# Attention and expert layer on one core: the attention's hand-planned order drawn up anew, with longer landing times of its DMA transpositions and loads

## The chip, the cores and the metric

The kernel runs on one core of a Trainium2 chip. The metric is the device time in microseconds of one execution, as the median of several runs; the kernel before takes 1341.63 us (three runs, 1341.21 to 1343.16). The engines of the core issue independently, each strictly in its own order, and wait for each other by semaphores: TensorE (PE in the profile, PEld for its weight loads), VectorE (DVE), ScalarE (ACT), GpSimd (POOL) and SyncE (SP), which here only issues DMAs.

## What is computed

An attention over 8 batches x 8 heads (576 positions of width 64) in which each query keeps its 32 largest scores, followed by a layer of eight experts, to which the 4608 tokens are assigned greedily by their gate's logits, with 576 tokens for each expert.

```python
def _attn_ref(q, k, v):                      # (8, 8, 576, 64) each
    scores = np.matmul(q, k.transpose(0, 1, 3, 2)) / np.sqrt(64)
    kth = np.partition(scores, -32, axis=-1)[..., -32:-31]
    scores = np.where(scores >= kth, scores, -1e9)
    attn = np.exp(scores - np.max(scores, axis=-1, keepdims=True))
    attn = attn / (np.sum(attn, axis=-1, keepdims=True) + 1e-09)
    return np.matmul(attn, v)

x = attention.transpose(0, 2, 1, 3).reshape(4608, 512)
# logits = x @ w_gate; pairs (token, expert) in falling order, 576 tokens an expert
out[token] = np.maximum(x[token] @ w1[e], 0) @ w2[e]
```

## The kernel before

The attention takes the heads in 32 pairs (`pairs`; index `n`), and a pair's queries in nine tiles of 128 rows: tiles 0 to 3 belong to the first head, 5 to 8 to the second, and tile 4 holds the 64 rows that are left of each. Values are split in a high and a low half of 16 bits, so that products of 16-bit numbers give the precision of 32 bits.

**Preparing a pair** (`prep`, lines 355 to 428, for pairs 1 to 31). SP loads keys and queries (`ldk`, `ldq`: lines 364 and 365, two DMAs each; `ldq` may not start ahead of `ldk`) and values (`ldv`, `ldw`: lines 368 and 370). ACT rounds the keys to 16 bits (`hk`, line 379) and the queries (`hq`, 378); POOL scales both (`gk`, `gq`, 383) and subtracts the rounded part, which gives the lower parts (`lk`, `lq`, 384). Then SP transposes the keys by DMA into `Kt` (`tk`, line 394, which needs `hk` and `lk`) and the queries into `Qt` (`tq`, line 394, which needs `hq` and `lq`). POOL copies a corner of `Kt` into `kz` (`kz`, line 396), and splits the values (`hv` 371, `gv` 374, `lv` 375). Both transpositions must have landed before the first scores of the pair.

**A tile** (`tile_ops`, line 429). PE computes the scores into PSUM (`s0`, `s1`, line 449); DVE takes the eight largest of each of six pieces (`c0` to `c5`, lines 453 and 454) and ranks the 48 candidates (`k0` to `k4`, lines 457 to 461); ACT marks by sign which scores exceed the 24th and counts them (`nt` 462, `sg` 466); DVE turns the count into a fill (`fl`, 476); PE takes the marked scores away (`o0`, `o1`, lines 471, 472 and 449, the latter with `kz`); DVE finds the next eight (`y8`, line 473) and ACT keeps what is left (`rl`, 479). After three tiles POOL copies their maxima into the query tile (`mo`, line 500) and SP transposes them (`q2`, line 501).

**The weights of a tile** (`soft`, line 503). PE adds up the transposed scores and masks (`ma`, `mb` 515; `ag0` to `ag3`, 520 and 521), ACT takes the exponential into a buffer `F` or `E` (`ex`, 525; `F` has four buffers in rotation), POOL splits it (`eh` 528, `el` 531; `el` frees the buffer). `tail` does the same for the last 64 keys (`tm` to `tc`, `te`, `th`, `tl`), `values` (line 597) multiplies with the values (`v0` to `v2`), `logits` computes the gate's logits for the pair.

**What sets the order.** Every operation is entered with a due time: the entry of the table `TAU` for its name and tile, plus `n` times `PER`. The last pair has entries of its own (with `_`). `Loom.run` (line 144) sorts each engine's operations by due time and lets the engine issue them in exactly that order; a due time is a place in the order, and delays nothing by itself. The planner keeps a clock of its own beside it, from the duration `d` and the landing time `late` (the time between the end of the issue and the use) of each operation. This clock decides the order in which the engines' instructions are written into the program and how many filling products PE gets in planned gaps (`stay`, line 346). The routing's first part is put behind the last pair (`pa`, `pb`). Then the expert layer follows with a planner of its own.

```python
        for op in sorted(self.ops, key=lambda o: o["t"])[::-1]:
            if op["e"]: lines[op["e"]].append(op)
```

Of the kernel before, what the change touches and what calls it, by code (L numbers as in the profile page):

```python
# [210 lines left out]
def attention(tc, q,k,v,w_gate,x_out,L,acc,cuts, pairs,ahead=()):  # L211
# [3 lines left out]
    with ExitStack() as ctx:  # L215
# [7 lines left out]
        V,G,A,T=nc.vector,nc.gpsimd,nc.scalar,nc.tensor  # L223
# [34 lines left out]
        def rims():  # L258
# [8 lines left out]
        PER=24.535894  # L267
        TAU=dict(ldk=[-36.532489], ldq=[-34.645812], hk=[0.490652], gk=[-24.714477], lk=[-5.646046], cq=[-5.038599], hq=[4.011956], gq=[-18.2134], lq=[-1.41611], tk=[-9.773551], 
            tq=[-4.444251], kz=[-1.095786], ldv=[-24.423458], ldw=[-15.183043], hv=[1.708939], gv=[1.465658], lv=[25.618464], 
            s0=[15.009426,17.614268,18.631424,22.361038,24.496034,25.814059,27.254638,33.349677,36.178074],   # L270
            s1=[16.343093,17.885021,20.327135,22.783661,26.664804,25.913004,28.409475,33.746851,36.209416], 
            c0=[15.654456,17.929975,19.415024,22.536798,25.246239,26.257597,28.63835,34.277851,36.041556], 
            c1=[17.465533,19.354973,19.526392,23.324677,26.510292,27.491491,30.464787,35.252934,36.134791], 
            c2=[16.14122,19.028081,20.113037,23.116345,26.52603,27.664486,31.6479,34.660167,36.642377], 
            c3=[17.439299,18.346588,19.614338,22.878597,26.109616,28.666317,30.753739,34.412699,36.484631], 
            c4=[17.433128,19.11846,19.726728,23.098966,25.671467,26.710686,30.311069,34.875005,36.785795], 
            c5=[17.596633,18.81432,20.666021,23.663524,27.350852,28.872828,29.897138,34.293634,36.846704], 
            k0=[17.656568,19.718444,21.338341,23.830734,27.576103,30.498137,31.893452,35.844752,37.524856], 
            k1=[17.901067,19.816894,21.373417,24.48664,28.321978,31.388234,31.971058,36.583722,38.053143], 
            k2=[18.064263,20.452465,21.832022,24.637402,28.778187,31.776554,32.244806,37.313756,38.482906],   # L280
            k3=[18.993761,21.078023,21.844845,25.194363,28.998044,31.961926,32.319626,38.002729,40.436698], 
            k4=[19.074582,21.339742,22.085206,25.227026,29.974125,32.191951,32.957171,38.220581,41.56231], 
            nt=[19.923862,21.07989,21.635673,25.254182,28.591256,32.027101,35.264635,38.85557,41.390678], 
            sg=[20.428927,21.387458,23.353451,27.967037,31.229058,33.065454,36.668009,40.650797,41.58337], 
            fl=[21.577768,23.681133,25.061496,28.688352,31.777369,33.560239,37.442546,41.651365,42.368937], 
            o0=[22.255713,23.476629,23.782874,29.486798,31.978369,34.185679,39.17079,40.855488,42.489752], 
            o1=[22.580295,23.758687,24.695984,29.602817,32.243463,35.167978,39.421143,40.990239,42.794684], 
            y8=[23.918204,24.466854,25.583237,31.427866,32.292299,35.365448,39.778219,42.173235,43.421626], 
            rl=[24.524765,24.674952,25.985548,31.889713,33.167469,37.480824,40.938297,43.094705,44.212375], mo=[17.22803,22.609648,32.244558], q2=[11.61061,18.819227,22.679302], 
            ma=[28.187642,28.949286,34.490254,37.224887,36.588764,41.036568,47.11078,43.383667,46.883924],   # L290
            mb=[28.23947,29.200388,34.68484,38.173395,37.181707,41.348337,47.186607,43.395459,47.135361], 
            ag0=[28.394948,29.705353,35.236427,38.677025,37.486884,41.916796,47.782677,43.90671,47.273045], 
            ag1=[28.459302,30.02036,35.766277,38.717047,37.66623,42.06767,48.090036,43.991452,47.55756], 
            ag2=[28.761553,30.046327,35.893568,38.829728,37.866094,42.091054,48.175398,44.686062,47.642137], 
            ag3=[28.897045,30.35191,35.899376,39.091561,38.127979,42.704103,48.27918,45.03561,47.820927], 
            ex=[30.703735,31.866723,36.101128,38.52712,38.229268,43.764389,48.909161,45.107316,48.482621], 
            eh=[30.707012,25.992076,30.410065,32.650788,0,35.796509,42.676563,41.704942,42.62945], 
            el=[33.507947,35.037032,32.484109,35.292126,0,36.976438,45.999822,46.502435,46.867538], cu=[43.086149], tm=[45.201666], tn=[45.828976], ta=[46.475366], tb=[46.487846], 
            te=[45.579953], th=[37.430026], tl=[41.594999], tc=[48.93781], tr=[49.863139], v0=[48.332202,48.464061,48.800604,49.234735,49.265037,49.318516,49.731533,50.138756], 
            n0=[50.382659], i0=[50.679088], x0=[50.554385,51.338797,51.396623,52.155786], v1=[50.538791,50.772288,51.395036,51.76531,51.787905], n1=[52.080784], i1=[52.839633],   # L300
            x1=[52.866022], v2=[55.191767,55.935243,56.126953,56.189534,57.051874,57.720408,57.831705,57.842499], n2=[57.42161], i2=[58.184646], 
            x2=[58.08899,58.376986,58.610975,60.544343], lt0=[64.108659], lt1=[64.320988], lt2=[64.321728], lt3=[65.107349], lc=[66.399674], ld0=[67.432455], ld1=[67.437679], 
            ld2=[67.516612], ld3=[67.572664], lp=[68.382371], rt0=[63.984394], rc=[63.180125], rd0=[64.630251], rd1=[65.022487], rp=[66.272452], st=[73.135698], ldk_=[-35.889897], 
            ldq_=[-35.188398], hk_=[0.616827], gk_=[-24.933336], lk_=[-5.038599], cq_=[-2.708316], hq_=[3.883817], gq_=[-20.049088], lq_=[0.195792], tk_=[-9.504837], tq_=[-4.870748], 
            kz_=[8.382132], ldv_=[-15.700575], ldw_=[-12.925284], hv_=[1.695369], gv_=[11.624079], lv_=[41.595099], 
            s0_=[14.912706,17.433233,18.631324,20.492929,24.453667,25.169692,26.759069,32.243563,35.872581], 
            s1_=[15.007788,17.854586,19.373458,21.992311,25.725414,26.77937,28.395048,34.185579,36.064346], 
            c0_=[15.536163,17.833143,19.614438,21.338441,24.723626,25.671567,26.799064,32.717003,35.943152], 
            c1_=[15.943341,19.702662,19.748862,23.522126,25.570329,25.678257,29.603343,32.771706,37.189612], 
            c2_=[16.351868,19.714023,20.612321,22.341619,24.926231,25.769041,28.558249,32.776643,36.041656],   # L310
            c3_=[17.439199,18.520609,20.318569,23.023736,25.194363,26.143094,27.405455,34.195478,37.584804], 
            c4_=[15.843145,19.604253,19.960156,23.738631,25.227026,25.852663,31.296853,32.8259,38.666525], 
            c5_=[15.715676,19.746815,20.561277,23.584636,25.922609,27.350852,30.641257,34.449493,37.7529], 
            k0_=[17.533337,20.305911,21.471646,24.034479,26.591582,27.638632,33.08639,35.365448,39.723553], 
            k1_=[17.656568,20.452465,21.577868,24.123414,26.916815,30.182078,33.972607,36.785795,40.096054], 
            k2_=[18.064163,20.610546,21.890349,24.43491,27.267468,30.99811,34.365495,38.053143,40.397585], 
            k3_=[18.648077,20.943324,22.268027,24.637402,27.491591,31.970958,35.156304,39.458481,41.787164], 
            k4_=[19.614338,21.373417,22.792541,25.42924,27.664486,32.243382,35.844652,39.778219,41.857785], 
            nt_=[19.923862,20.954933,23.353451,25.362363,28.111171,31.3086,35.264635,40.289699,41.800716], 
            sg_=[20.234342,22.563689,23.830252,25.725512,30.106172,33.065454,37.551336,40.654704,42.614537],   # L320
            fl_=[21.832022,23.081535,23.955728,27.266875,30.540837,35.252834,41.302682,42.882482,42.882582], 
            o0_=[22.083337,23.307503,23.743286,28.180748,32.214938,35.994341,39.561765,42.194735,42.684328], 
            o1_=[22.509549,23.601583,23.862297,28.720863,32.243463,36.058538,40.2929,42.539638,42.789509], 
# [16 lines left out]
            pb_=[0,0,0,0,0,0,0,0,96.391443,0,0,121.358085,0,0,0,0,0,121.468485])  # L340
# [14 lines left out]
        def prep(n):  # L355
# [61 lines left out]
            def go(name,*a,**kw): return at((n,name,0),*a,**kw)  # L417
# [11 lines left out]
        def tile_ops(P,i):  # L429

            n=P["n"]
            def go(name,*a,i=i,**kw): return at((n,name,i),*a,**kw)
# [987 lines left out]
```

## Time and profile before

| what | value |
|---|---|
| median of three runs | 1341.63 us |
| the profiled execution, its own time | 1338.39 us |
| its span, first to last instruction | 1336.6 us |
| PE busy | 1242.4 us (93%) |
| DVE busy | 1096.9 us (82%) |
| ACT busy | 929.5 us (70%) |
| POOL busy | 818.5 us (61%) |
| mean granted clock of TensorE | 0.968 of full speed |

The attention takes the span to about 885 us; the expert layer follows. All times are in us from the span's start unless marked. A row of the timeline is one instruction, or several alike in a row (x2 and so on): its start, its duration, engine, line, operation, output<-input, shape, and in brackets how long the engine stood idle before it and whose work ended that. For SP the duration is that of issuing; the data lands later, which is seen at the instruction whose wait "DMA Kt<-nk" or "DMA Qt<-nq" ends. A row by stretches gives the length of the stretch, the busy time (and count) of each engine in it, the granted TensorE clock, the busy share of the DMA engines, and GB/s.

### The profile page before, as it was taken

Reading aid. Unit: us, or ns where it says so; the run is one execution under the profiler, and the core shown is the slowest. Engines: PE = TensorE matmul, PEld = TensorE weight load, DVE = VectorE, ACT = ScalarE, POOL = GpSimd, SP = SyncE. Lnnn points to the kernel's source line nnn. Section 1 sums busy time; section 2 is a strip of 40 time slices with the busy share of each in tenths; the row PEclk is TensorE's granted clock in tenths of the full one; section 3 lists DMA queues with packets and bytes.
Section 4 is the critical chain, followed back from the end, with each engine's and each line's share of the span. In section 5 each row is a group of like instructions: output and inputs, shape, how many; then the busy total and the mean of one; then the engine's idle time right before and its main releaser. Section 6 shows DMA issues by size and latency. Waiting matters only on the chain. (4 is left out here: it accounts for less than half of the span.)

```text
span 1336.6 us, 45657 instructions
## 1 busy us (share of the span) xinstructions
PE 1242.4 (93%) x17268; PEld 929.4 (70%) x17269; DVE 1096.9 (82%) x5557; ACT 929.5 (70%) x2177; POOL 818.5 (61%) x1090
## 2 busy tenths in 40 slices
PE   7889998999999898999999898986989999999998
PEld 6677776777777776777778677775756755765664
DVE  7989898998999898998989798948989998972420
ACT  3889898898999897998989898841534542442421
POOL 3798788888898788889878888732033231141011
PEclk9999899999999998999989899986989999999999
DMA  5644475455455645466446445314456665684001
GB/s 114 109 84 76 92 144 80 82 132 95 90 118 97 107 82 113 95 103 120 82 88 144 82 85 110 51 40 136 164 154 167 208 205 180 182 233 130 17 29 38
DMA packets 313133, 148.99 MB, mean 111 GB/s; under 512 B 278533, under 2 KB 294917, under 8 KB 311877
## 3 DMA queue, kind: packets, MB, share of 16 engines
q1 hardware_dynamic: 306530, 126.53, 44.3%
q0 software_dynamic: 5968, 19.14, 4.6%
q8 instruction: 137, 2.24, 0.7%
q14 instruction: 96, 0.78, 0.2%
q10 hardware_dynamic: 402, 0.29, 0.1%
HBM read 71.60 MB, written 18.87 MB: 68 GB/s over the span
## 5 line engine op out<-in xcount | busy, mean ns | idle before, releaser
L453 DVE MAX8 cd<-s 128x8 f32<-128x96 f32 x1440 | 308.6, 251 | 68.3 <-PE s L449 62.3
L449 PE MATMUL s<-Kt,Qt 128*128 128x64 f16 (+3 forms) x1600 | 273.6, 275 | 45.3 <-DMA Qt<-nq 43.1
L531 POOL TENSOR_TENSOR elm<-F,ehm 128x512 f16<-128x512 f32 x253 | 287.4, 1156 | 2.8
L449 PEld LDWEIGHTS <-Qt 128*128 128x128 f16 (+1 forms) x1920 | 141.6, 103 | 123.8 <-DMA Qt<-nq 47.5
L479 ACT ACTIVATE r<-s,st 128x576 bf16<-128x576 f32 x288 | 209.7, 740 | 24.0 <-DVE st L473 22.2
L466 ACT ACTIVATE w<-s,st 128x576 uint16<-128x576 f32 x288 | 213.7, 742 | 17.3 <-PE s L449 9.4
L473 DVE MAX8 st<-s 128x8 f32<-128x584 f32 x288 | 216.7, 762 | 3.7 <-PE s L472 3.1
L1269 PE MATMUL ph<-xT,w1h 128*128 128x288 f16 (+1 forms) x1024 | 190.7, 286 | 2.8 <-DMA xT<-xs 2.8
L1329 POOL DMA_INDIRECT out_dram<-ob,idx x39 | 42.7, 1095 | 238.5 <-ACT ob L1324 221.9
L521 PE MATMUL pt<-Qt,Kt 65*128 65x128 f16 (+1 forms) x1280 | 179.0, 217 | 2.5 <-DMA Qt<-nq 2.4
L520 PE MATMUL pt<-Qt,Kt 128*128 128x128 f16 (+1 forms) x1280 | 179.5, 216 | 0.0
L525 ACT ACTIVATE F<-pt 128x512 f32<-128x512 f32 x256 | 151.0, 594 | 20.1 <-PE s L472 8.5
L471 PE MATMUL s<-w,off 128*128 128x512 f16 x576 | 157.2, 293 | 1.9 <-ACT w L466 1.9
L528 POOL TENSOR_SCALAR ehm<-F 128x512 f16<-128x512 f32 x253 | 154.1, 618 | 5.8 <-ACT F L525 5.6
L1269 PE MATMUL ph<-xT,w1l 128*128 128x288 f16 (+1 forms) x512 | 146.4, 287 | 0.0
L521 PEld LDWEIGHTS <-Kt 65*128 65x128 f16 x1280 | 119.4, 99 | 8.9 <-issue 2.3
L622 PE MATMUL pv<-vh,ehm 128*128 128x65 f16 x1012 | 118.0, 195 | 3.9 <-ACT F L525 0.8
L520 PEld LDWEIGHTS <-Kt 128*128 128x128 f16 x1280 | 118.6, 99 | 3.6 <-issue 3.2
L622 PE MATMUL pv<-vl,ehm 128*128 128x65 f16 x1012 | 118.2, 193 | 0.0
L622 PE MATMUL pv<-vh,elm 128*128 128x65 f16 x1012 | 118.2, 193 | 0.0
L515 PE MATMUL pt<-out__184,r 128*128 128x128 bf16 (+1 forms) x1280 | 113.4, 216 | 1.6 <-ACT F L525 0.5
L622 PEld LDWEIGHTS <-ehm 128*128 128x128 f16 x2024 | 106.5, 98 | 12.0 <-issue 7.5
(314 smaller groups left out, 3502.6 us busy)
## 6 DMA issues: line engine op xcount, KB each, us to landing
wr<-in_moe_w_dram SPq DMA_DIRECT2D x32, 1024.0 KB
kn<-in_k_dram SPq DMA_DIRECT2D x32, 256.0 KB
vt<-in_v_dram SPq DMA_DIRECT2D x64, 128.0 KB
x<-xb SPq DMA_DIRECT2D x8, 1024.0 KB
qn<-in_q_dram SPq DMA_DIRECT2D x31, 256.0 KB
Qt<-nq SPq DMA_TRANSPOSE x129
kn<-in_k_dram SPq DMA_DIRECT2D x32, 32.0 KB
vt<-in_v_dram SPq DMA_DIRECT2D x64, 16.0 KB
```

Of the source, the lines that this page charges most:

```text
L449: part(at_(),kind,T.matmul(o[rows],P[Q][:n_,qc],P[K][:n_,k0(h):k0(h)+o.shape[1]],start=first,stop=last,skip_group_check=True),"P")
L453: if c<5: part(at_(),"o",V.max(o,main(512-CW-CW*c,512-CW*c) if u else main(CW*c,CW*c+CW)),"V")
L466: part(at_(),"m",A.activation(D["w"],span(0,576),AF.Sign,bias=P["st"][:,i,32:33],scale=(1+2.0**-21),accum_out=acc[:,col]),"A")
L471: part(at_(),"o" if half else "t",T.matmul(span(o,o+n_),off,P["w"][i][:,o:o+n_],start=False,stop=bool(half),skip_group_check=True),"P")
L473: def next8(): part(at_(),"m",V.max(P["st"][:,i,24:32],span(-8,576) if side() else span(0,584)),"V")
L479: part(at_(),"m",A.activation(r,span(0,576),AF.Relu,bias=P["st"][:,i,31:32],scale=-1.0),"A")
L520: T.matmul(o,K2[:,kb:kb+128],Q1[:,qc],start=False,stop=False,skip_group_check=True)
L521: T.matmul(o,K3[0:65,kb:kb+128],Q2[0:65,qc],start=False,stop=(c==3 and h==sub[-1][0]),skip_group_check=True)
L528: G.tensor_scalar(D["eh"],D["E"],1.0,0.0,op0=ALU.mult,op1=ALU.add)
L531: G.tensor_tensor(el,D["E"],D["eh"],op=ALU.subtract); P["e"][i]=(D["eh"],el)
L622: for m_ in (range(N-3) if part==0 else range(N-3,N)): T.matmul(out,seq[m_][0],seq[m_][1],start=(m_==0),stop=(m_==N-1))
L1269: P.matmul(B["ph"][:,lo-c0:hi-c0],a[:,c,fs],xT[:,b+c,lo:hi],start=(i==0),stop=(i==11),skip_group_check=True)
```

## The change

All due times of the attention's table are replaced, the period `PER` goes from 24.535894 to 24.599358, and the calls for the DMAs get other times: the landing times `late` of `tk` go from 2.2 to 3.3, of `tq` from 1.7 to 3.1, of `q2` from 1.7 to 2.3, of `ldk` from 3.1 to 3.3, of `ldv` and `ldw` from 2.8 to 3.0; the issue times `d` of `tk` from 2.65 to 2.7 and of `tq` from 3.4 to 3.2. No operation is added or removed, and none gets another predecessor. What each does is untouched; only the place of each in its engine's order, and the planner's own clock.

Sorted by due time, the operations of SP stand in this order, repeated for each pair (`n` is the pair that is being transposed; `q2[0]` is for tiles 0 to 2):

```
before: q2[0](n-1)  ldk(n+1)  ldq(n+1)  tk(n)  q2[1](n-1)  tq(n)  q2[2](n-1)  ldv(n+1)  ldw(n+1)
after:  q2[0](n-1)  tk(n)  q2[1](n-1)  tq(n)  ldq(n+1)  q2[2](n-1)  ldv(n+1)  ldw(n+1)  ldk(n+2)
```

and those of POOL (m is the pair whose tiles are being ranked; n = m+1):

```
before: mo[0](m) eh[8] eh[6] cu(m-1) lk(n) cq(n) el[6] el[7] el[8](m-1) mo[1](m) lq(n) kz(n) gk(n+1) lv(m) eh[1](m) gv(n)
        hv(n) eh[2] eh[0](m) gq(n+1) mo[2](m) el[2] eh[3] el[0] el[1] el[3] eh[5] el[5] th tl eh[7](m)
after:  mo[0](m) cq(n) eh[6] eh[8](m-1) lk(n) el[6](m-1) cu(m-1) el[7](m-1) mo[1](m) lq(n) el[8](m-1) eh[1](m) gk(n+1) hv(n)
        el[1](m) lv(m) eh[0](m) gv(n) mo[2](m) eh[2](m) gq(n+1) eh[3] el[2] el[0] el[3](m) kz(n) eh[5] el[5] th tl eh[7](m)
```

On PE, DVE and ACT neighbouring operations change places by a few positions; ACT still issues `hk(n)` directly behind `rl` of tile 1 of pair m.

The core of the diff (the entries of the names above, and all changed calls):

```diff
-        PER=24.535894
-        TAU=dict(ldk=[-36.532489], ldq=[-34.645812], hk=[0.490652], gk=[-24.714477], lk=[-5.646046], cq=[-5.038599], hq=[4.011956], gq=[-18.2134], lq=[-1.41611], tk=[-9.773551], 
-            tq=[-4.444251], kz=[-1.095786], ldv=[-24.423458], ldw=[-15.183043], hv=[1.708939], gv=[1.465658], lv=[25.618464], 
-            s0=[15.009426,17.614268,18.631424,22.361038,24.496034,25.814059,27.254638,33.349677,36.178074], 
...
-            c0=[15.654456,17.929975,19.415024,22.536798,25.246239,26.257597,28.63835,34.277851,36.041556], 
...
-            k0=[17.656568,19.718444,21.338341,23.830734,27.576103,30.498137,31.893452,35.844752,37.524856], 
...
-            y8=[23.918204,24.466854,25.583237,31.427866,32.292299,35.365448,39.778219,42.173235,43.421626], 
-            rl=[24.524765,24.674952,25.985548,31.889713,33.167469,37.480824,40.938297,43.094705,44.212375], mo=[17.22803,22.609648,32.244558], q2=[11.61061,18.819227,22.679302], 
...
-            ex=[30.703735,31.866723,36.101128,38.52712,38.229268,43.764389,48.909161,45.107316,48.482621], 
-            eh=[30.707012,25.992076,30.410065,32.650788,0,35.796509,42.676563,41.704942,42.62945], 
-            el=[33.507947,35.037032,32.484109,35.292126,0,36.976438,45.999822,46.502435,46.867538], cu=[43.086149], tm=[45.201666], tn=[45.828976], ta=[46.475366], tb=[46.487846], 
...
+        PER=24.599358
+        TAU=dict(ldk=[-26.046356], ldq=[-11.217283], hk=[1.693157], gk=[-16.476817], lk=[2.113881], cq=[-0.281183], hq=[5.377492], gq=[-7.319096], lq=[4.998426], tk=[7.438771], 
+            tq=[9.05314], kz=[17.492607], ldv=[-5.369609], ldw=[-5.252506], hv=[8.361196], gv=[12.68533], lv=[35.426233], 
+            s0=[14.516299,17.080675,19.728065,21.701037,25.872458,27.685112,29.321663,34.707657,36.266651], 
...
+            c0=[15.539793,18.367327,20.182255,23.431638,26.935083,28.75464,30.619492,35.241827,36.68286], 
...
+            k0=[18.184904,20.132195,22.288982,26.021141,30.281411,30.342436,32.220511,37.44161,38.717671], 
...
+            y8=[25.030351,25.184346,27.079939,32.137918,34.321734,36.578467,39.228175,42.686039,43.258665], 
+            rl=[25.524121,25.92131,27.808239,34.376082,34.683205,36.898688,39.474093,44.176364,44.427874], mo=[24.306907,29.571582,39.218295], q2=[31.510491,32.891024,39.159573], 
...
+            ex=[30.884883,32.288299,36.575642,37.029821,36.972388,44.354733,48.656101,45.114639,49.749406], 
+            eh=[35.943962,32.57108,41.219802,41.923763,0,43.703947,49.049745,48.781724,50.14471], el=[41.984966,34.554876,41.9434,42.07828,0,46.115281,52.018076,53.61198,56.065712], 
...
-            lk=go("ldk",lambda: loads("k",k),o2,order=[prev["lv"]],e="D",d=1.28,late=3.1); l=go("ldq",lambda: loads("q",q),[],order=[lk],e="D",d=1.25,late=3.1)
+            lk=go("ldk",lambda: loads("k",k),o2,order=[prev["lv"]],e="D",d=1.28,late=3.3); l=go("ldq",lambda: loads("q",q),[],order=[lk],e="D",d=1.25,late=3.1)
-            b_=go("tk",lambda: turn("K"),[h1,k2]+p2,e="D",d=2.65,late=2.2)
-            c=go("tq",lambda: turn("Q"),[h2,q2],order=[b_],e="D",d=3.4,late=1.7)
+            b_=go("tk",lambda: turn("K"),[h1,k2]+p2,e="D",d=2.7,late=3.3)
+            c=go("tq",lambda: turn("Q"),[h2,q2],order=[b_],e="D",d=3.2,late=3.1)
-            lv=go("ldv",loadv,p3,order=[l],e="D",d=1.28,late=2.8); P["lv"]=lw=go("ldw",loadw,[],order=[lv],e="D",d=1.28,late=2.8); P["lds"]=at((n,"",0),lambda: None,[lv,lw])
+            lv=go("ldv",loadv,p3,order=[l],e="D",d=1.28,late=3.0); P["lv"]=lw=go("ldw",loadw,[],order=[lv],e="D",d=1.28,late=3.0); P["lds"]=at((n,"",0),lambda: None,[lv,lw])
-                a=go("mo",most,[P["mx"][j] for j in range(i0,i+1)],e="G",d=.245,i=i0//3); P["q2"][i0//3]=go("q2",q2,[a],e="D",d=1.25,late=1.7,i=i0//3)
+                a=go("mo",most,[P["mx"][j] for j in range(i0,i+1)],e="G",d=.245,i=i0//3); P["q2"][i0//3]=go("q2",q2,[a],e="D",d=1.25,late=2.3,i=i0//3)
```

## Rows read from the trace of the kernel before

**Rows 1.** VectorE instructions: start, us, engine, line, operation, shapes, [idle before <-releaser]

```profile
480.03 1.45 DVE L473 MAX8 st<-s 128x8 f32<-128x584 f32 x2
...
496.58 0.27 DVE L453 MAX8 cd<-s 128x8 f32<-128x96 f32 x1 [0.92 <-PE s L449]
```

**Rows 2.** All 30 stretches: length, busy PE, PEld, DVE, ACT, POOL, clock, DMA, GB/s

```profile
52.86:861.44 808.58, 753.32 (x12902) 598.81 (x12899) 728.98 (x4278) 721.82 (x1786) 686.93 (x929) 0.97 0.53 100
```

**Rows 3.** TensorE's longest wait: us in total, times, longest

```profile
PE s L449 <- DMA Qt<-nq: 43.1, 28, 2.9
```

**Rows 4.** Two of 18 stretches with a timely `tk`, and their sum

```profile
107.38:131.88 24.50, 24.02 (x431) 19.19 (x428) 24.05 (x144) 23.66 (x60) 21.90 (x29) 1.00 0.53 99
...
481.48:506.87 25.39, 23.75 (x419) 18.89 (x415) 24.08 (x143) 23.96 (x60) 21.14 (x28) 1.00 0.68 142
...
sum 458.98, PE 437.44 PEld 348.25 DVE 435.77 ACT 431.13 POOL 396.11; mean PE 24.30 PEld 19.35 DVE 24.21 ACT 23.95 POOL 22.01
```

**Rows 5.** Two of 12 stretches with a late `tk`, and their sum

```profile
294.06:322.46 28.40, 26.47 (x445) 21.13 (x445) 24.46 (x145) 24.31 (x61) 24.39 (x35) 0.94 0.45 86
...
506.87:537.74 30.87, 27.60 (x445) 21.61 (x445) 24.68 (x145) 24.48 (x61) 24.73 (x36) 0.89 0.50 79
...
sum 349.60, PE 315.88 PEld 250.56 DVE 293.21 ACT 290.70 POOL 290.82; mean PE 26.32 PEld 20.88 DVE 24.43 ACT 24.22 POOL 24.24
```

**Rows 6.** GpSimd instructions of two pairs, in order of time

```profile
483.54 1.29 POOL L384 TENSOR_TENSOR nk<-sck,nk 128x576 f16<-128x576 f32 x1 [1.40 <-ACT st L462]
...
488.34 1.29 POOL L384 TENSOR_TENSOR nq<-scq,nq 128x576 f16<-128x576 f32 x1
...
492.32 0.29 POOL L396 TENSOR_SCALAR kz<-Kt 64x128 f16<-64x128 f16 x1 [2.68 <-DMA Kt<-nk]
...
500.18 3.38 POOL L531 TENSOR_TENSOR elm<-F,ehm 128x512 f16<-128x512 f32 x3
...
507.76 0.20 POOL L500 TENSOR_SCALAR nq<-st 128x3 f16<-128x3 f32 x1
...
509.29 1.28 POOL L384 TENSOR_TENSOR nk<-sck,nk 128x576 f16<-128x576 f32 x1
...
519.37 0.29 POOL L396 TENSOR_SCALAR kz<-Kt 64x128 f16<-64x128 f16 x1 [4.01 <-DMA Kt<-nk]
```

**Rows 7.** SyncE's DMA issues of the same two pairs: start, us of issuing

```profile
484.85 3.66 SPq L394 DMA_TRANSPOSE Kt<-nk  x1
...
488.63 1.18 SPq L501 DMA_TRANSPOSE Qt<-nq  x1
...
489.90 3.30 SPq L394 DMA_TRANSPOSE Qt<-nq  x1
...
507.99 1.22 SPq L501 DMA_TRANSPOSE Qt<-nq  x1
...
509.26 0.58 SPq L364 DMA_DIRECT2D kn<-in_k_dram  x1
...
511.02 0.55 SPq L365 DMA_DIRECT2D qn<-in_q_dram  x1
...
511.68 3.60 SPq L394 DMA_TRANSPOSE Kt<-nk  x1
...
516.66 3.73 SPq L394 DMA_TRANSPOSE Qt<-nq  x1
```

**Rows 8.** TensorE instructions: first products of pairs, and one that reads `kz`

```profile
309.73 0.39 PE L449 MATMUL s<-Kt,Qt 128*128 128x512 f16 x1 [1.77 <-DMA Qt<-nq]
...
495.87 0.60 PE L449 MATMUL s<-Kt,Qt 128*128 128x512 f16 x2 [1.05 <-DMA Qt<-nq]
...
503.94 0.19 PE L449 MATMUL s<-kz,Qt 128*128 128x64 f16 x1
...
523.97 1.03 PE L449 MATMUL s<-Kt,Qt 128*128 128x512 f16 x2 [2.49 <-DMA Qt<-nq]
```

**Rows 9.** ScalarE instruction: the exponential of the sixth tile of a pair

```profile
499.66 0.60 ACT L525 ACTIVATE F<-pt 128x512 f32<-128x512 f32 x1
```

126 lines of the change are left out of this document (63 added, 63 removed).

## Prediction

> **What bounds the kernel now.** I read the stretches first, then PE's waits, then one late and one timely pair instruction by instruction. The attention works through 32 pairs of heads with one repeating order, so I cut it at one mark per pair: the end of the second `next8` of a pair, the DVE row that ends at 481.48 [rows 1]. From the mark of pair 1 to that of pair 31 lie 30 stretches, 808.58 us, 26.95 us each, and in them PE is busy 753.32 us and DVE 728.98 [rows 2]. Both are nearly full, so a gain must come from idle time on both at once. The list of waits shows where that is: PE waits 43.1 us for the transposed queries `Qt`, in 28 pairs, the longest entry of that list [rows 3].
>
> The stretches fall into two kinds. In 18 of them the transposition of the keys is issued within 0.25 us of the end of the instruction it needs; they average 25.50 us, PE's granted clock is 1.00 in each, and the shortest is 24.50 [rows 4]. In the other 12 that issue comes 0.5 to 1.9 us late; they average 29.13 us, and in ten the granted clock is 0.89 or 0.94 [rows 5]. The excess of the second kind over the first is 12 x (29.13 - 25.50) = 43.6 us. That is what can be won without shortening anything.
>
> Now one of each. Timely (mark 481.48): ACT rounds the keys, POOL makes their lower part `lk`, which waited 1.40 us for ACT and ends at 484.83 [rows 6]; SP issues the transposition `tk` at 484.85, `q2` at 488.63, `tq` at 489.90 [rows 7]; PE starts pair 18 at 495.87 after 1.05 us idle [rows 8], DVE at 496.58 after 0.92 idle [rows 1]. The chain takes 15.10 us, and DVE had 14.18 us of other work to cover it. Late (mark 506.87): `mo` ends only at 507.96 and `lk` did not wait, because POOL itself was late [rows 6]; SP issues the first `q2` at 507.99, then the four loads to 511.57, and `tk` at 511.68, 1.11 us after `lk` ended at 510.57 [rows 6, 7]. PE starts at 523.97, 17.10 us after the mark against 14.39: 1.44 us from the later `tk`, 1.34 from the slower landing of `tq` (7.31 against 5.97), -0.07 between [rows 7, 8]. This stretch is 5.48 us longer than the other (30.87 against 25.39), so another 2.77 us are lost behind the landing, and there its clock is 0.89 [rows 4, 5]: PE stood 2.49 us, its clock fell to the 1.2 GHz level for a part of the stretch, and DVE then waited for PE. The point lies between 1.05 us of idling, which kept the clock at 1.00, and 1.77, which ended in 0.94 [rows 4, 5, 8].
>
> Why POOL was late: it stood at `kz`, which copies a corner of the transposed keys, 2.68 us in pair 18 and 4.01 in pair 19, waiting for `Kt` to land [rows 6]. POOL issues in order, and after the first of these waits it had no idle time left before the `lk` of pair 19.
>
> **The change part by part.** Each engine issues in the order of the due times, so sorting the two tables gives both orders.
>
> *Loads on SP.* Before, between the first `q2` and `tk` stand four load issues, 509.26 to 511.57: 2.3 us [rows 7]. After, the key loads stand behind the value loads, by the due times 8 us ahead of `q2`, and the query loads behind `tq`; `tk` follows `q2` directly. In the 18 timely stretches SP is through with the loads before `lk` ends, so this is worth nothing there; in the late ones 1.1 us of the 1.44. `tk` may also get shorter without loads ahead (3.66 against 3.30 for `tq`, the same size with none ahead [rows 7]): between 0 and -0.36 us a pair; I take 0, since it was 3.60 in the late pair too.
>
> What I weigh against this: the query loads now go out right behind `tq`, and may slow its landing. No row shows a load right behind a transposition. A `tk` right behind two pairs of loads had landed 7.47 us after its issue (484.85 to the release of `kz` at 492.32), a `tq` with none ahead 5.97 [rows 6 to 8]: 1.50 us for two, so half, 0.75, bounds one; 0 is the other end, since data issued later need not pass data issued earlier. I take 0. The Trainium skill, "DMA: Bandwidth & Descriptors", says in "Queues, rings and completion order" that each DMA engine consumes descriptors in the order of its ring, which would give 0; in "Issuing engines are not separate DMA queues" it says that all DMAs share the 16 engines and interleave, which would give a part of the 0.75 and leads to the fourth rival. No row here tells the two apart.
>
> *`kz` on POOL.* It moves from right behind `lq` to behind 15 more operations. The wait of 2.68 or 4.01 us goes, for `Kt` has landed by then. What is late next? Before, POOL did the same operations without a wait from `kz` (492.32) to 503.56 [rows 6]: 11.24 us. Less `kz` (0.29), plus the `el` of the last tile, which moves behind `lq` (1.13, as one of the three at 500.18), that is 12.08 us from the end of `lq` at 489.63: `kz` runs at 501.7 to 502.0. PE first needs it at 503.94 [rows 8], so 1.9 us remain: price 0, and 1 us for each us that POOL is later than that. POOL then enters the next pair 2.7 us earlier, and `lk` waits for ACT as in the timely stretches.
>
> *The chain itself is not shortened.* `rl`, `hk`, `lk`, `tk`, `q2`, `tq`, landing, first products: the same operations with the same predecessors in both orders. Two `el` instead of three stand between `lk` and `lq`, so `lq` may end up to 1.1 us earlier, but `tq` is issued 0.09 us after `q2` frees SP (489.81 to 489.90 [rows 7]), so SP sets it, not `lq`. So the 1 us of idling in a timely pair stays, and I let the 18 timely stretches stand.
>
> *The order on the other engines.* The `el` of tile 0 moves from far ahead to near the exponential of tile 5, which by the rotation of four buffers writes where tile 0's stood. By the reckoning above it ends at 500.6; the exponential started at 499.66 [rows 9], and its due time moves 0.65 us later against the first chunk's. So ACT may wait between 0 and 0.3 us there, and a late query load in front of `gq` could add a few tenths on POOL: 0 to 0.8 us a pair together, the distance from 499.66 to 500.6 being the far end. I take 0.1 a pair, 3 us, since the due times leave the near end likelier. The last pair's own order and the routing work behind it change; I take 0, bounded by 2 us either way, twice the distance between the shortest stretch and the timely mean [rows 4]. The longer landing times in the calls change only the planner's own clock.
>
> **The sum.** Against the profiled execution (1338.39 us, its span 1336.6): 1338.39 - 43.6 + 3 = 1297.8. The median of the runs is 1341.63, 3.24 above the profiled one, so the forecast is 1301 us. With the ends: -11 for a shorter `tk` (30 x 0.36), +21 for the far end of ACT's wait (30 x 0.7): 1288 to 1324.
>
> **The rivals.**
> 1. *No wait is left.* If the landing comes 1 us sooner, every stretch is like the shortest, 24.50 [rows 4]: 30 x (26.95 - 24.50) = 73.5, so 1268. For it: it has happened, at 107.38. Against: nothing in the chain gets shorter. 0.10.
> 2. *POOL becomes the bound.* It is busy 22.01 us of a timely 25.50 and 24.24 of a late 29.13 [rows 4, 5]; in the new order `kz`, `el` and `gq` stand close to their users. If POOL is still late in half of the 12 pairs, half the gain is left: 1341.6 - 21.8 = 1320. 0.20.
> 3. *The change doesn't do what it says.* The wait for `Qt` hangs on operations that it doesn't touch, so the same stalls come at other pairs: 1338 to 1345. Against: the late pairs have a cause, and it is removed. 0.04.
> 4. *Slower: the query loads hold back the landing of `tq`.* With 0.75 us more, the 1.05 us of a timely pair becomes 1.80, beyond the point where the clock fell. It decides where more than 12 of the 30 pairs are over it: with 18 it costs 6 x 3.63 = 22 us, so 1363, with all 30 1407. For it: the loads sit in front of the last bytes of the step everything waits for. Against: a load is issued only when `tq` is wholly issued. 0.11.
>
> **How the numbers follow.** The forecast has 0.55, with 1288 to 1324 as its own range. The range to 8 in 10 takes in the second rival and a part of the first, and leaves out the fourth: 1278 to 1336. A measurement of this kernel can tell some 0.2%, 2.7 us, from no change. Faster by more: forecast, first and second rival, 0.85. Within: most of the third, 0.04. Slower by more: the fourth, 0.11.
>
> **What would show it.** Right: the granted clock at 1.00 in all stretches, each near 25.5; PE's wait for `Qt` down from 43.1 to some 25 us; no row in which POOL waits for `Kt`; `tk` at the end of `lk` in every pair. The chain wrong: stretches near 24.5 and no wait for `Qt`. Rival 2: rows in which PE waits for `kz`, or ACT for `el`. Rival 4: `tq` to landing above 6.7 us with a granted clock below 1.00 in most stretches.

## The result, and the profile after

The kernel after takes 1271.16 us (1270.99 to 1271.54) beside 1341.42 (1340.40 to 1343.16) of the kernel before on the same chip: a ratio of 0.9475, 95% interval 0.9459 to 0.9492. The forecast was 1301, its range 1278 to 1336. The time lies below the range, where the first rival stood (1268). The profiled execution took 1270.99 us with a span of 1269.2. Lines of the kernel after are those of before less one from the table of due times on.

The same cut, at the end of the second `next8` of each pair, gives these stretches (columns as in [rows 2]: length, busy PE, PEld, DVE, ACT, POOL, clock, DMA, GB/s):

```profile
51.18:792.26 741.08, 727.70 (x12894) 586.66 (x12894) 715.97 (x4279) 713.09 (x1785) 686.65 (x927) 1.00 0.53 108
```

and, of the 30, a typical one, two of the longest, and the one that is followed below:

```profile
174.15:198.84 24.69, 24.66 (x439) 19.77 (x436) 24.05 (x144) 23.92 (x61) 23.88 (x36) 1.00 0.51 99
...
272.54:298.14 25.60, 24.98 (x447) 20.18 (x447) 23.89 (x144) 23.84 (x61) 24.95 (x37) 1.00 0.47 97
...
495.20:519.79 24.59, 24.02 (x431) 19.40 (x429) 23.75 (x143) 23.73 (x60) 22.39 (x30) 1.00 0.51 98
...
766.32:792.26 25.94, 24.80 (x441) 19.99 (x441) 24.39 (x146) 23.92 (x60) 21.82 (x29) 1.00 0.42 71
```

The 30 stretches take 741.08 us against 808.58 [rows 2], 67.5 less; the spans differ by 67.4. So all of the gain lies in the repeating part. The mean is 24.70 us against 26.95, every stretch has a granted clock of 1.00, and the longest is 25.94, where a late one had taken 29.13 on the mean [rows 5]. PE is now busy 98% of the stretches.

The waits from 60 to 830 us (engine, line, what it waited for: us in total, times, longest):

```profile
POOL nk L383 <- ACT nk L378: 27.0, 27, 1.4
...
POOL scq L382 <- DMA qn<-in_q_dram: 15.0, 21, 1.9
...
PE s L448 <- DMA Qt<-nq: 5.0, 7, 1.1
...
DVE cd L452 <- PE s L448: 4.4, 8, 0.9
```

PE's wait for `Qt`, 38.2 us in the same window before (43.1 in the whole run [rows 3]), is nearly gone. In this part of the run no row has POOL waiting for `Kt` at `kz` any more; one new wait is there, POOL at `gq` for the query loads. How it stands in one pair, SP first (start, us of issuing; compare [rows 7]):

```profile
494.81 1.23 SPq L500 DMA_TRANSPOSE Qt<-nq  x1
498.42 2.65 SPq L393 DMA_TRANSPOSE Kt<-nk  x1
501.17 1.20 SPq L500 DMA_TRANSPOSE Qt<-nq  x1
502.47 3.31 SPq L393 DMA_TRANSPOSE Qt<-nq  x1
505.82 0.58 SPq L363 DMA_DIRECT2D qn<-in_q_dram  x1
```

then POOL and PE (compare [rows 6] and [rows 8]):

```profile
497.11 1.28 POOL L383 TENSOR_TENSOR nk<-sck,nk 128x576 f16<-128x576 f32 x1 [1.12 <-ACT nk L378]
...
500.95 1.29 POOL L383 TENSOR_TENSOR nq<-scq,nq 128x576 f16<-128x576 f32 x1
502.19 1.17 POOL L530 TENSOR_TENSOR elm<-F,ehm 128x512 f16<-128x512 f32 x1
...
510.65 0.67 POOL L382 TENSOR_SCALAR scq<-qn 128x576 f32<-128x576 f32 x1 [0.91 <-DMA qn<-in_q_dram]
```

```profile
508.79 0.61 PE L448 MATMUL s<-Kt,Qt 128*128 128x512 f16 x2 [0.46 <-DMA Qt<-nq]
```

`lk` ends at 498.39, `tk` goes out at 498.42 and takes 2.65 us to issue, not 3.66. The second `q2` follows at 501.17, and SP could issue `tq` at 502.37; `lq` ends at 502.24. `tq` goes out at 502.47, 7.27 us behind the mark at 495.20, against 8.42 us in the timely pair of before (489.90 less 481.48). PE idles 0.46 us and not 1.05.

The table gives the means over the 30 stretches of this kernel, of before and of the experiments, in us behind the mark. "First product" is the start of the first product of the next pair's first tile, 128x512. "Extra" are the filling products (`stay`) in these stretches; before and after have none there, and a shorter or longer planned gap changes their number.

| kernel | `tk` out | issuing `tk` | `lq` ends | `tq` out | first product | PE idle before it | stretch | extra |
|---|---|---|---|---|---|---|---|---|
| before | 3.91 | 3.66 | 8.23 | 9.11 | 15.06 | 1.31 | 26.95 | 0 |
| b_kz | 3.45 | 3.59 | 8.14 | 8.63 | 14.69 | 1.17 | 26.31 | 0 |
| b_loads | 3.37 | 2.85 | 8.14 | 8.44 | 14.02 | 0.54 | 26.20 | 394 |
| b_loads_kz | 3.39 | 2.81 | 8.16 | 8.53 | 14.04 | 0.40 | 26.09 | 394 |
| b_loads_kz_el | 3.50 | 2.81 | 7.88 | 8.00 | 14.09 | 0.09 | 25.52 | 30 |
| b_early_kz_el | 3.37 | 2.82 | 7.61 | 7.80 | 13.86 | 0.12 | 25.15 | 0 |
| b_pool_sp2 | 3.37 | 2.80 | 7.60 | 7.74 | 13.89 | 0.11 | 25.17 | 0 |
| b_late | 3.86 | 3.60 | 8.21 | 9.00 | 15.11 | 0.79 | 26.48 | 233 |
| after | 3.24 | 2.82 | 7.11 | 7.51 | 13.41 | 0.18 | 24.70 | 0 |
| a_loads_back | 3.39 | 3.68 | 7.05 | 8.57 | 14.42 | 1.08 | 25.97 | 0 |
| a_ldq_back | 3.22 | 2.97 | 7.06 | 7.64 | 13.38 | 0.21 | 24.65 | 0 |
| a_ldq_early2 | 3.22 | 2.77 | 7.05 | 7.43 | 13.29 | 0.14 | 24.59 | 0 |
| a_el_back | 3.26 | 2.80 | 8.19 | 8.60 | 14.49 | 0.44 | 25.60 | 284 |
| a_kz_back | 3.22 | 2.81 | 7.04 | 7.48 | 15.60 | 0.03 | 26.97 | 0 |

### The profile page after: what moved, and what is told of

Its sections match the earlier page's. It is cut to its first block, busy times and chain, and to the rows that moved or that the text cites. A ratio compares the mean times of both kernels' runs of the same rounds, so it can differ in the third digit from the quotient of the medians.

```text
span 1269.2 us, 45619 instructions
## 1 busy us (share of the span) xinstructions
PE 1216.1 (96%) x17274; PEld 916.9 (72%) x17275; DVE 1084.0 (85%) x5557; ACT 920.6 (73%) x2177; POOL 819.8 (65%) x1090
## 5 line engine op out<-in xcount | busy, mean ns | idle before, releaser
L530 POOL TENSOR_TENSOR elm<-F,ehm 128x512 f16<-128x512 f32 x253 | 290.5, 1159 | 2.8
L448 PE MATMUL s<-Kt,Qt 128*128 128x64 f16 (+3 forms) x1600 | 269.1, 268 | 9.1 <-DMA Qt<-nq 7.3
L448 PEld LDWEIGHTS <-Qt 128*128 128x128 f16 (+1 forms) x1920 | 134.6, 101 | 77.8 <-issue 32.7
L470 PE MATMUL s<-w,off 128*128 128x512 f16 x576 | 148.8, 286 | 7.6 <-ACT w L465 7.5
L1268 PEld LDWEIGHTS <-w1h 128*128 128x128 f16 x1024 | 95.0, 98 | 29.0 <-issue 5.8
L1297 ACT ACTIVATE hh<-ph 128x288 f16<-128x288 f32 x128 | 52.3, 410 | 85.6 <-PE ph L1268 79.3
```

Source lines behind the costliest of these rows:

```text
L448: part(at_(),kind,T.matmul(o[rows],P[Q][:n_,qc],P[K][:n_,k0(h):k0(h)+o.shape[1]],start=first,stop=last,skip_group_check=True),"P")
L530: G.tensor_tensor(el,D["E"],D["eh"],op=ALU.subtract); P["e"][i]=(D["eh"],el)
L1268: P.matmul(B["ph"][:,lo-c0:hi-c0],a[:,c,fs],xT[:,b+c,lo:hi],start=(i==0),stop=(i==11),skip_group_check=True)
```

## The experiments

Each kernel is one of the two with entries of the table changed, in b_late the calls instead; entries of the last pair (with `_`) are changed alike where the edit needs it. Ratios are to the kernel before on the same chip (medians there 1333 to 1337 us), in brackets their 95% intervals.

### The kernel before with up to four names moved

**b_loads**: all loads leave their place between the first `q2` and `tk`; the key loads go ahead, the query loads behind `tq`.

```diff
-ldk=[-36.532489], ldq=[-34.645812]
+ldk=[-38.5], ldq=[-27.5]
```

> The kernel before, with the key and query loads alone moved on SP to where the change puts them. Theory L (load descriptors in front of a transposition hold up its issue): the issue of `tk` falls from 3.6 to some 2.8 us and it follows `lk` in every pair; `tq` is then set by `lq`, some 8.2 us after the mark instead of 8.4 to 11; `kz` still waits for `Kt`, but shorter. 1311 us (1300 to 1322). Rival K (all of it is POOL's wait at `kz`): issue of `tk` stays at 3.6, 1330 to 1341. Rival O (the order on PE, DVE and ACT made the difference): 1335 to 1341.

Measured: 1315.6 us, 0.9883 (0.9815 to 0.9952). The issue of `tk` falls from 3.66 to 2.85 us although nothing about `tk` itself is touched, and it follows `lk` in every pair. What sets `tq` now is POOL. In all 30 pairs the second `q2` waits for its `mo`, which stands directly in front of `lq` behind three `el` and ends at 6.90, while the issue of `tk` had ended at 6.22; that `q2` frees SP at 8.35, `lq` ends at 8.14, and `tq` goes out at 8.44. A new wait is there, the query loads that land late for `gq`. From 60 to 830 us:

```profile
POOL scq L383 <- DMA qn<-in_q_dram: 45.8, 28, 3.7
...
PE s L449 <- DMA Qt<-nq: 13.0, 17, 2.2
```

The time lies in the range of theory L, but not only for its reason: the part of a stretch behind the first chunk takes 11.42 us, and 10.52 in those stretches of before in which the clock stays at 1.00. The 394 filling products stand there, 11 or 16 in all stretches but the last, 0.6 to 0.9 us of PE. The wait at `gq` looks like the lesser cause: b_loads_kz_el has nearly the same (41.8 us) with 30 filling products, and its part behind the first chunk takes 10.64 us. Neither was tried by itself.

**b_kz**: `kz` alone moves to its place of after.

```diff
-kz=[-1.095786]
+kz=[10.8]
```

> The kernel before, with `kz` alone moved on POOL to where the change puts it, behind the lower part of tile 3. Theory L together with the recorded reckoning: POOL no longer waits for `Kt`, so no pair is late, but `tk` still takes 3.6 us to issue behind the loads and the 1 us of idling stays: 1298 us (1290 to 1306), granted clock near 1.00. Rival K: all the gain, near 1271. Rival O: 1330 to 1341.

Measured: 1315.88 us, 0.9864 (0.9788 to 0.9940). POOL's wait at `kz` is gone and `tk` goes out at 3.45, timely in 28 of 30 pairs. Yet PE's wait for `Qt`, 38.2 us in this window before, is hardly smaller:

```profile
PE s L449 <- DMA Qt<-nq: 34.8, 25, 3.3
```

This is what the prediction's main step asked for, a `tk` on time, and it gave 0.64 us of the 2.25 us a pair. With `tk` still issued right behind the loads, seven stretches keep a clock of 0.89 or 0.94. The time lies in none of the three ranges.

**b_loads_kz** makes both moves, **b_loads_kz_el** also puts the last tile's `el` behind `lq`, as after.

```diff
-46.502435,46.867538], cu=
+46.502435,47.7], cu=
```

> The kernel before with both moves. Theory L: `tk` issues in 2.8 us, `tq` is set by `lq` at 8.2 us after the mark, so only 0.2 us of the chain is won over `kz` alone, and the landings are steadier: 1290 us (1283 to 1298). Rival K: as `kz` alone. Rival O: above 1320.

> The kernel before with both moves, and the lower part of the last tile moved behind `lq` on POOL as in the change. Theory L: `lq` ends some 7.7 us after the mark and `tq` is issued at 7.8, so 0.4 to 0.6 us a pair less than with the two moves: 1278 us (1272 to 1286). Rival K: as `kz` alone. Rival O: above 1290, since PE, DVE and ACT keep their old order.

Measured: 1310.28 us, 0.9852 (0.9781 to 0.9923), and 1289.97, 0.9677 (0.9609 to 0.9745). Both are slower than theory L had it. Without the `el` POOL waits 73.1 us for the query loads at `gq`, and 394 filling products stand in the stretches, as in b_loads. With it `tq` goes out 0.53 us earlier and PE's idle time before the first product falls from 0.40 to 0.09 us, but the first product itself comes no earlier (14.09 beside 14.04). The 0.57 us by which the stretches fall lie behind the first chunk (10.64 us beside 11.30), where 30 filling products and not 394 are left. So this pair of runs does not price the `el`; a_el_back, below, does.

**b_early_kz_el** puts the query loads right behind the key loads, with the other two moves kept.

```diff
-ldk=[-36.532489], ldq=[-34.645812]
+ldk=[-38.5], ldq=[-38.0]
```

> The kernel before with four names moved: both loads far ahead, behind the value loads, so that POOL need not wait for the query loads at `gq`; `kz` behind the lower part of tile 3; the lower part of the last tile behind `lq`. Theory L: these three moves are nearly the whole change: 0.955 of the kernel before (0.948 to 0.962), POOL without waits for loads or for `Kt`. Rival O: the old order on PE, DVE and ACT keeps it above 0.965, as with the query loads behind `tq`.

Measured: 1282.71 us, 0.9610 (0.9559 to 0.9661). The wait at `gq` is gone, and PE waits 3.6 us for `Qt` in all. Four moved names give 1.80 of the 2.25 us a pair.

### The kernel after with one step taken back

**a_kz_back**: `kz` stands right behind `lq` again.

```diff
-kz=[17.492607]
+kz=[5.05]
```

> The kernel after with `kz` put back right behind `lq`, as before. The prediction's theory (K: a wait at `kz` makes GpSimd late for the next `lk`): GpSimd waits 0.5 to 2.5 us for `Kt` in each pair, `lk` starts without a wait for ScalarE in some pairs and `tk` goes out late there: 1285 us (1278 to 1300). Rival (T: since `Kt` now lands 1 to 2 us sooner, the wait is short and GpSimd catches up): 1272 us (1269 to 1276), `lk` ends at 3.2 to 3.3 us behind the mark in nearly every pair.

Measured: 1336.48 us, 1.0021 (0.9992 to 1.0050): one instruction of 0.29 us, put back, takes the whole gain. But not in the way that either theory had. `tk` and `tq` go out as early as in the kernel after, and PE hardly waits for `Qt` (0.03 us a pair). The waits from 60 to 830 us:

```profile
DVE rs L593 <- PE pv L621: 54.8, 29, 3.0
PE pv L621 <- POOL elm L530: 53.5, 29, 2.9
POOL kz L395 <- DMA Kt<-nk: 52.8, 28, 2.9
```

and one pair, POOL, PE and DVE:

```profile
514.86 1.27 POOL L383 TENSOR_TENSOR nq<-scq,nq 128x576 f16<-128x576 f32 x1
518.93 0.29 POOL L395 TENSOR_SCALAR kz<-Kt 64x128 f16<-64x128 f16 x1 [2.79 <-DMA Kt<-nk]
519.19 1.15 POOL L530 TENSOR_TENSOR elm<-F,ehm 128x512 f16<-128x512 f32 x1
```

```profile
520.39 0.20 PE L621 MATMUL pv<-vh,elm 128*128 128x65 f16 x1 [2.78 <-POOL elm L530]
...
520.80 0.59 PE L448 MATMUL s<-Kt,Qt 128*128 128x512 f16 x2
```

```profile
521.00 0.16 DVE L593 TENSOR_SCALAR rs<-pv 128x4 f32<-128x4 f32 x1 [2.78 <-PE pv L621]
```

POOL waits at `kz` for 2.79 us; the `el` of the pair before, which after's order has right behind, waits with it; PE's product with the values needs that `el` and stands 2.78 us; DVE's `rs` stands 2.78 us behind it. The products at 520.80 are the scores of the old pair's last tile but one; they are queued behind the values on PE, and so is all that follows, to the first product of the new pair at 526.83, 17.72 us behind the mark (15.60 on the mean, 13.41 in the kernel after). One wait is passed on whole through three queues, and ten stretches have a clock of 0.94. So with `el` where after has it, `kz` had to move too: the two moves belong together.

**a_loads_back**: the four loads stand again between the first `q2` and `tk`.

```diff
-ldk=[-26.046356], ldq=[-11.217283]
+ldk=[-17.6], ldq=[-17.4]
```

> The changed kernel, with the key and query loads alone put back on SP between the first `q2` and `tk`, where they were before. Theory L (loads in front of the transposition hold up its issue): `tk` issues in 3.5 us instead of 2.7, `tq` goes out some 8.2 us after the mark instead of 7.3, and PE idles about 1 us for `Qt` in most pairs, now and then long enough for the clock to fall: 1300 us (1288 to 1315). Rival O (the order on the other engines made the difference): 1268 to 1276.

Measured: 1311.72 us, 0.9850 (0.9786 to 0.9914). `tk` goes out 0.15 us later on the mean, but takes 3.68 us instead of 2.82, so `tq` goes out 1.06 us later, PE idles 1.08 us, and in six stretches the clock is below 1.00. A pair with one of the longest issues:

```profile
497.42 1.23 SPq L500 DMA_TRANSPOSE Qt<-nq  x1
498.69 0.58 SPq L363 DMA_DIRECT2D kn<-in_k_dram  x1
...
500.46 0.55 SPq L364 DMA_DIRECT2D qn<-in_q_dram  x1
501.15 4.77 SPq L393 DMA_TRANSPOSE Kt<-nk  x1
```

**a_ldq_back**: only the query loads go back there.

```diff
-ldq=[-11.217283]
+ldq=[-17.4]
```

> The changed kernel with the query loads alone put back in front of `tk`; the key loads stay far ahead. Theory L with a dose: `tk` issues in some 3.1 us, half of the way, and half of the time is lost: 1285 us (1277 to 1295). If only the pair of loads right in front counts, `tk` takes 3.5 us and the time is that of both loads put back. Rival O: 1268 to 1276.

Measured: 1270.74 us, 0.9531 (0.9479 to 0.9584), stretches of 24.65: no loss, where theory L had expected half of that of a_loads_back. (The time lies in the range of rival O; that the loads count all the same, b_loads and a_loads_back show.) Two load issues end at 498.15, `tk` waits for `lk` until 499.53, and takes 2.76 us:

```profile
496.94 0.58 SPq L363 DMA_DIRECT2D qn<-in_q_dram  x1
497.57 0.58 SPq L364 DMA_DIRECT2D qn<-in_q_dram  x1
499.53 2.76 SPq L393 DMA_TRANSPOSE Kt<-nk  x1
```

So a load ahead of `tk` as such matters little; four of them that end 0.14 us ahead do (and four that end 0.46 us ahead in the timely pair of before, 484.39 to 484.85, with 3.66 us), two that end 1.4 us ahead hardly do. Distance and number were not tried apart, but the pairs of this run tell something: in six of them the two loads end only 0.11 to 0.58 us ahead, and `tk` takes 3.08 us on the mean (2.85 to 3.33), beside 2.91 in those with 0.74 to 1.40 us; four loads that end 0.11 to 0.47 us ahead go with 3.33 to 4.33 us in before. So the number counts, and more than the distance.

**a_el_back**: the last tile's `el` goes back in front of `mo[1]` and `lq`.

```diff
-52.018076,53.61198,56.065712],
+52.018076,53.61198,53.8],
```

> The kernel after, with one entry changed: the lower part `el` of the last tile stands again in front of `mo[1]` and `lq` on GpSimd (1.1 us). If `lq` is what sets `tq` once `tk` is short (theory C): `lq` ends 8.1 to 8.3 us behind the mark instead of 7.1, `tq` is issued at 8.3 to 8.5 instead of 7.5, TensorE stands 0.4 to 1.0 us for `Qt` in most pairs, the stretches average 25.2 to 25.6, and the time is 1288 us (1280 to 1298). If SP alone sets `tq` (the prediction's step, N): no change from the kernel after, 1271 (1268 to 1275).

Measured: 1293.84 us, 0.9676 (0.9645 to 0.9706), in the range of theory C: `lq` ends at 8.19, `tq` goes out at 8.60, the stretches take 25.60. One pair, SP and POOL:

```profile
515.92 2.62 SPq L393 DMA_TRANSPOSE Kt<-nk  x1
519.65 1.18 SPq L500 DMA_TRANSPOSE Qt<-nq  x1
520.92 3.54 SPq L393 DMA_TRANSPOSE Qt<-nq  x1
```

```profile
517.17 2.28 POOL L530 TENSOR_TENSOR elm<-F,ehm 128x512 f16<-128x512 f32 x2
519.41 0.21 POOL L499 TENSOR_SCALAR nq<-st 128x3 f16<-128x3 f32 x1
519.57 1.28 POOL L383 TENSOR_TENSOR nq<-scq,nq 128x576 f16<-128x576 f32 x1
```

`lq` is only one of two gates. The second `q2` also stands behind the `el`: SP is free at 518.54, `mo` ends at 519.62, `q2` goes out at 519.65 and frees SP at 520.83; `lq` ends at 520.85. So it is in all 30 pairs (`mo` ends at 6.95, the issue of `tk` at 6.05), and which of `q2` and `lq` ends later changes from pair to pair. In the kernel after, `mo` ends at 5.82, and `q2` follows the issue of `tk` without a wait. This edit moves both gates and does not tell them apart. All 30 keep a clock of 1.00, with 284 more filling products, and the first product comes 1.08 us later, so the 0.90 us are the chain's, not the clock's.

**a_ldq_early2**: the query loads go right behind the key loads, well ahead of the first `q2` (the words below have them in front of the key loads); **after_again** is the kernel after on the same chip.

```diff
-ldq=[-11.217283]
+ldq=[-26.0]
```

> The kernel after with the query loads a place earlier than `q2[0]`, in front of the key loads, and not behind `tq`; the same program as the earlier run of this edit, now beside the kernel after on one chip. If a load behind `tq` holds back the landing of `Qt`: 2 us or more faster than the kernel after. If it costs only GpSimd's short wait at `gq` (0.5 us a pair, mostly beside other work): 0 to 3 us faster, 1269 (1267 to 1272).

> The kernel after, unchanged, beside the others on this chip: 1271 us (1269 to 1273), 0.946 to 0.950 of before.

Measured: 1267.45 us (1265.73 to 1268.67), 0.9492 (0.9447 to 0.9537), and 1268.65 (1264.24 to 1274.07), 0.9499 (0.9443 to 0.9554). No load is left behind `tq`, and the stretches are 24.59 beside 24.71: 0.12 us a pair, too little for these medians to tell. An earlier run of the same edit gave 1266.84, 0.9495 (0.9443 to 0.9547). It is the shortest version seen, and not shown to beat the kernel after.

### What is left: three engines, and the planner's clock

**b_pool_sp2**: the kernel before with the whole order of POOL and SP of after. (A first such mixture, b_pool_sp, at 1298.61 us, had `mo[1]` behind `lq` because the two kernels differ in `PER`; it tested something else. The reverse, a_pool_sp, at 1353.64, made waits of its own, DVE 43.9 us for products that now came late, and tells nothing.)

```diff
-... lk=[-5.646046], ... lq=[-1.41611], tk=[-9.773551], ... kz=[-1.095786], ...
+... lk=[2.108427], ... lq=[4.985531], tk=[7.41958], ... kz=[17.447478], ...
...
```

> The kernel before, with the exact order of GpSimd and SP of the kernel after (in the first such mixture `mo[1]` had come to stand behind `lq`, so that the second `q2` went out 1.0 us late). The other three engines keep the order of before; no filling products are added. Theory S (all of the gain lies in the order of GpSimd and SP): stretches of 24.7, as the kernel after, ratio to it 0.998 to 1.003, 1271 us. Theory X (the last part lies in the order of TensorE, VectorE and ScalarE): stretches of 25.0 to 25.2, 1281 us (1277 to 1288), no wait for `Qt` left, the first product at 13.3 us or later behind the mark.

Measured: 1283.04 us, 0.9602 (0.9556 to 0.9648), stretches of 25.17. On the same chip the kernel after took 1268.65: 14.4 us, or 0.48 us a pair, lie in the order of PE, DVE and ACT, or in the planner's own clock, in which the two also differ (neither has filling products in the stretches). They lie ahead of the pair's first product (13.89 and 13.41). No wait for `Qt` is behind it (PE idles 0.11 us). The largest waits of this kernel at that place are

```profile
DVE rs L594 <- PE pv L622: 10.0, 28, 0.5
...
PEld L622 <- POOL elm L531: 9.3, 28, 0.5
```

some 0.36 us a pair, in which the values wait for the `el` that now comes later. In the kernel after the values' first product stands 1.1 us later (`v0` 49.46 and not 48.33 in the table), and from 60 to 830 us no row has PE waiting for an `el`. That this is most of the 0.48 us is read from the rows and was not tried by itself.

**b_late**: the kernel before with its table untouched; only the landing and issue times in the seven calls are those of after.

```diff
-            b_=go("tk",lambda: turn("K"),[h1,k2]+p2,e="D",d=2.65,late=2.2)
+            b_=go("tk",lambda: turn("K"),[h1,k2]+p2,e="D",d=2.7,late=3.3)
...
```

> The kernel before with its table of due times untouched; only the landing and issue times of the seven calls are those of the kernel after. If only the order of the engines counts (the prediction): as the kernel before, ratio 0.998 to 1.002, 1341 us (1338 to 1344). If the planner's own clock counts by itself, through the order in which the instructions are written and the filling products: off by more than 4 us either way, with another number of TensorE instructions in the stretches.

Measured: 1322.28 us, 0.9902 (0.9867 to 0.9938), though every engine's own work stands as before. The planner expects longer gaps and puts filling products into them, 233 in the stretches, as here:

```profile
119.57 0.61 PE L346 MATMUL pt<-out__184 128*128 128x128 bf16 x8
122.74 1.03 PE L449 MATMUL s<-Kt,Qt 128*128 128x512 f16 x2 [2.56 <-DMA Qt<-nq]
```

The chain is as long as before (first product at 15.11 beside 15.06, first chunk at 15.87 in both), but only 5 stretches have a clock below 1.00 instead of 10, and the part behind the first chunk takes 10.61 us and not 11.09: 0.48 us a pair, 14.4 us, came back with the clock. In before that part takes 12.23 us in the ten stretches in which the clock fell, and 10.52 in the others. In the kernel after this plays no part: it has no filling product in its stretches, as before had none.

## Why the prediction was wrong, by its own steps

**Right.** No late stretch is left, and with them their excess of 43.6 us went; `tk` goes out 0.02 us behind `lk`; the clock is 1.00 in all 30; POOL waits for `Kt` nowhere in these stretches, and PE never waits for `kz`; the end behind the last mark is 1.8 us longer (476.94 against 475.16), within the 2 us set for it. The query loads behind `tq` cost 0.12 us a pair at most as far as the stretches tell (a_ldq_early2 beside after_again, not clear of the noise), so the fourth rival falls, for which 0.75 was the bound. Of the two sentences of the Trainium skill, "DMA: Bandwidth & Descriptors", weighed there, the order of the ring ("Queues, rings and completion order") agrees with that; the interleaving showed no cost for `tq` that is clear of the noise.

**Wrong, first: "the chain itself is not shortened".** Two terms. The issue of `tk` was let stand ("I take 0", bound -0.36); it fell by 0.84 us, from 3.66 to 2.82. The bound came from `tq`, the same size with no loads ahead; but `tq` takes 2.9 to 3.3 us on the mean in every kernel of the table, 3.16 before and 3.23 after, and is no measure for `tk`. b_loads and a_loads_back show in both directions that it is the loads right ahead. The timely row with 3.66 also had loads ahead, finished before `lk` ended; "worth nothing there" looked only at when `tk` starts. And "SP sets it, not `lq`" stopped one step short: what holds SP there is `q2`, and `q2` needs `mo`, which stands behind the same `el` as `lq`. This is its row in the timely pair before:

```profile
488.18 0.21 POOL L500 TENSOR_SCALAR nq<-st 128x3 f16<-128x3 f32 x1
```

`mo` had ended at 488.39 and the issue of `tk` at 488.51 [rows 7], so POOL was 0.12 us from being the gate; with `tk` 0.84 us shorter it is (b_loads), unless the `el` moves too. Moving it brings `mo` and `lq` 1.1 us forward, and putting it back costs 0.90 us a pair (a_el_back). With both terms `tq` goes out at 7.51 us and not at 8.41, the mean of the timely pairs before (7.27 and 8.42 in the two pairs shown): nearly the "1 us sooner" on which the first rival hung. Its "against", that nothing in the chain gets shorter, was this same mistake.

**Wrong, second: "I let the 18 timely stretches stand".** All 30 stretches now take 24.70 us on the mean, 0.80 less than the timely ones had: 24 us. By b_pool_sp2 some 0.33 us of this are POOL's and SP's (25.50 to 25.17), and 0.48 are the order of the other three engines or the planner's clock; the forecast passed over that order as changes by a few positions. The sum is then 1297.8 - 24.0, less the 3 us for ACT's wait (measured: two waits, 0.7 us in all), which is 1270.8, beside 1270.99; since it is put together from the measured stretches, this says only that no other part of the run moved.

**Half right: POOL's lateness as the one cause.** It made `tk` late in twelve pairs, but b_kz, with `tk` timely in 28 of 30 pairs, keeps 34.8 us of PE's wait and an idle of 1.17 us a pair, and wins 19 us in the stretches and not 43.6: pairs with a timely `tk` also idle long enough there for the clock to fall. Nor is there one length of idling that decides, as the prediction's point between 1.05 and 1.77 us has it: a stretch of b_kz with 2.60 us keeps 1.00, another with 1.84 us has 0.94. A price of 0 for the new place of `kz` was right; what the old place would have cost beside the moved `el` was not seen: the whole gain (a_kz_back).

**Right only for this table:** that the landing times change only the planner's clock. b_late shows that the clock of the planner reaches the chip, and with it 1% of the time, through filling products as far as the rows show.

## What to carry to other kernels

Where a chain passes over two engines that end nearly together, shortening one shows little until the other is shortened too: take the gates one behind the other, and ask of each step what would set its start if it came 1 us sooner. The duration of a DMA's issue is not a property of the DMA alone; compare it with and without transfers issued right ahead before it is let stand in a sum. Before an instruction that may wait is put somewhere, list what is queued behind it there, on its engine and on those that wait for these: 0.29 us of work cost 68 us here (1336.48 beside 1268.65 on one chip).

## What the runs showed of the hardware

- A transposition of 128x2304 16-bit values, the keys', took SP 2.82 us to issue on the mean with no load right ahead (2.65 to 3.54, the kernel after), and 3.66 to 3.68 with four loads issued just ahead (before and a_loads_back; up to 4.82). From the end of the issue to the release of a waiting `kz` it took 3.02 us before (2.1 to 4.3, 29 pairs) and 2.88 in a_kz_back (1.5 to 4.1, 29 pairs), and from the start of the issue 6.69 and 5.69, so the landing moves with the issue.
- Idle gaps before the pair's first product of 1.77 us and more went with stretches at a clock of 0.94 or 0.89 in the kernel before (1.72 us with 0.94, 1.74 with 1.00); in b_kz one of 2.60 us went with 1.00. With 233 filling products ahead of first chunks that come as late as before, 5 stretches and not 10 fell below 1.00 (b_late): those with gaps of 2.09 to 2.56 us, while four with 1.81 to 1.96 us kept 1.00.
